# v of two batches loaded in four-token runs and unshuffled on TensorE, w_in in two halves, and a new order for slots 0 to 8

## The chip, the core and the metric

The kernel runs on one core of a Trainium2 chip. The engines of the core are TensorE (PE, with its weight loads shown as PEld), VectorE (DVE), ScalarE (ACT), GpSimd (POOL) and SyncE (SP), which here only issues transfers. Each engine has its own queue and works through it strictly in order; engines wait for one another and for transfers through semaphores. The metric is the device time in microseconds. Before the change it is 322.87 us, the median of three runs (322.14 to 323.13).

## The reference

Two layers run one after the other:

```
# q, k, v: (8 batches, 8 heads, 576 tokens, 64), fp32
scores = q @ k^T / 8 ; key j is seen by query i where 0 <= i - j < 128
scores += slope[h] * -(i - j)          # slope[h] = 2^-(h+1)
x = softmax(scores) @ v                # -> (4608 tokens, 512 = 8 heads * 64)
h = x @ w_in                           # w_in (512, 2048)
g = h * clip(h + 3, 0, 6) / 6
out = g @ w_out                        # w_out (2048, 512), out (4608, 512) fp32
```

## The kernel before

**Slots.** Attention is worked in 32 slots: slot g is batch g // 4 and head pair g % 4. Tokens lie in five blocks of 128 (the last has 64). For a slot, TensorE forms transposed scores for the diagonal blocks (`scd`) and for the blocks one off the diagonal (`sco`); ScalarE takes the exponential into `pd` and `po`; TensorE multiplies these by v, which has a column of ones beside each head (`vbuf`, 65 columns a head), so that one result holds both the weighted sum and its divisor; VectorE divides (`avs`); and five transposes with a copy put the slot into `xT`, the input of the second layer. In batch 0 the bias and the mask are added as table matmuls (`tables_diag`, `tables_off`) and `exp_full` takes 1024 columns at once; in later slots a bias column and a GpSimd select do this work, wholly or in part. From slot 8 on all scores of a slot go to one tile `sce` in 64x64 quarters (`scores`, L364 and L372).

**Second layer.** The tokens are cut in nine tiles nt of 512. For each nt there are 16 "up" units (four 512-column matmuls against `w_in`, L501, then ScalarE at L520 and VectorE at L521) and 16 "down" units (four 512-column matmuls against `w_out`, L551; four units make 128 rows of the output). `fill(n)` emits the next n units of a fixed list, if their tokens are in `xT`.

**PSUM.** There are eight banks: two tiles of two banks (`sc`), two tiles of one bank (`h`), one (`av`) and one (`o`). A tile can be written again only when its reader is done.

**Loading.** q and k of batch 0 come as nine-token runs (2304 bytes, `load_run`, L92), of batches 1 and 2 likewise (`load_double`, L98). v comes by tokens (`load_tokens`, L112): a descriptor for each token and head, 256 bytes. SyncE issues these in order, with eight completion lanes; a ninth transfer waits for the first. `w_in` comes through GpSimd's queue as four column quarters of 512 (`load_w_in`, L166), `w_out` as four row quarters (`load_w_out`, L171). Both are cast to bf16 on the way. Up unit ms needs w_in's columns 128 ms to 128 ms + 127.

**Order.** Everything is recorded by hand with `tc.manual_schedule`: `first_batch`, `second_batch`, then `segment(2 * NP, G)`, one slot an iteration. What stands in an engine's queue is the order of these calls. In `first_batch`, slots 0 to 3 go through transposes, scores and exponentials, then v is cast to bf16 (`cast_v`, L181), then `attend` (values of the slot in one `sc` tile) and `back` follow slot by slot; the first up units and the transposes of batch 1 (`wide_double`, L254) come after.

Of the kernel before, what the change touches and what calls it, by code (L numbers as in the profile page):

```python
# [18 lines left out]
def kernel(  # L19
# [29 lines left out]
    NB_FULL = 2  # L49
    RING = 4 * S  # L50
# [5 lines left out]
    ident = perm.tile([128, 128], BF16)  # L56
    bias3 = perm.tile([128, 1], FP32)
# [22 lines left out]
    p4buf = [held.tile([128, 2, 128], BF16, name=f"p4buf{i}") for i in range(2)]  # L80
# [94 lines left out]
    def second_w_in():  # L175
        nc.gpsimd.memset(w_out_sb[:, 4, 0:1], 0.0)
        load_w_in(1)

# [24 lines left out]

    def prepare(g, copies):
        for nm, copy in zip("qk", copies):
            pr = prs.tile([128, RT * D], BF16, tag=f"pr{nm}", name="pr",
                          padded_shape=[128, 2 * RT * D])
            copy(out=pr, in_=runs[nm][:, g % NP, :])
            st[g, nm] = pr

    def transposes(g, copies):
        b, hp = divmod(g, NP)
        for nm, dst, copy in (("q", qTb[b % 2], copies[0]), ("k", kTb[b % 2], copies[1])):
            src = st.pop((g, nm))
            tp = ps_h.tile([128, RT, RP], BF16, tag="h", name="tp", padded_shape=[128, 16, 64])
            for t in range(RT):
                for e in range(2):
                    r = slice(e * D, (e + 1) * D)
                    nc.tensor.transpose(tp[r, t, :], src[r, ts(t, D)], ident[r, r])
            copy(out=dst[:, hp, :, :].rearrange("p j c -> p (j c)")[:, 0:S].rearrange(  # L220
                "p (a t) -> p a t", t=RT), in_=tp.rearrange("p t a -> p a t"))
# [52 lines left out]
    def rooms(g):  # L274
        b, hp = divmod(g, NP)
        if full(g):
# [66 lines left out]
    def scores(g):  # L343
        if full(g):
            scores_diag(g)
            scores_off(g)
            return
# [4 lines left out]
        if g == 2 * NP:  # L352
# [31 lines left out]
    def exp_diag(g, e):  # L384
        h = 2 * (g % NP) + e
        pd = st[g, "pd"]
        if not full(g):
            nc.scalar.activation(out=pd[:, e, :, :], in_=st["sce"][e][:, :, 0, :],  # L388
                                 func=ACT.Exp, bias=bias_d[:, h:h + 1], scale=scale)
            mask_diag(g, e)  # L390
            return
        sc = st[g, "scd"]
        if diag_tabled(g):
            if e == 0:
                nc.scalar.activation(out=pd.rearrange("p e j c -> p e (j c)"), in_=sc,
                                     func=ACT.Exp, scale=scale)
            return
        nc.scalar.activation(out=pd[:, e, :, :].rearrange("p j c -> p (j c)"),
                             in_=sc[:, e, :], func=ACT.Exp,
                             bias=bias_d[:, h:h + 1], scale=scale)  # L400
        mask_diag(g, e)

    def mask_diag(g, e):
        pd = st[g, "pd"]
        nc.gpsimd.affine_select(out=pd[:, e, :, :], in_=pd[:, e, :, :],  # L405
                                pattern=[[0, 4], [1, 128]], channel_multiplier=-1, base=0,
                                compare_op=ALU.is_ge, fill=0.0)

    def exp_off(g, e):
        h = 2 * (g % NP) + e  # L410
        po, sc, p4 = st[g, "po"], st["sce"][e], p4buf[g % 2]
        nc.scalar.activation(out=po[:, e, :, :], in_=sc[:, :, 1, :], func=ACT.Exp,  # L412
                             bias=bias_o[:, h:h + 1], scale=scale)
        nc.gpsimd.affine_select(out=po[:, e, :, :], in_=po[:, e, :, :],  # L414
                                pattern=[[0, 4], [-1, 128]], channel_multiplier=1, base=-1,
                                compare_op=ALU.is_ge, fill=0.0)
        nc.scalar.activation(out=p4[:, e, 0:64], in_=sc[:, 3, 1, 64:128], func=ACT.Exp,  # L417
                             bias=bias_d[:, h:h + 1], scale=scale)
        if e == 1:
            nc.gpsimd.affine_select(out=p4[:, :, 0:64], in_=p4[:, :, 0:64],  # L420
                                    pattern=[[0, 2], [1, 64]], channel_multiplier=-1, base=0,
                                    compare_op=ALU.is_ge, fill=0.0)

    def av_matmuls(g, qts, where):
        b, hp = divmod(g, NP)
        vb = vbuf[b % 2]
        pd, po, p4 = st[g, "pd"], st[g, "po"], p4buf[g % 2]
        for qt in qts:
            for e in range(2):
                h = 2 * hp + e  # L430
                out_av = where(qt, e)
                if qt > 0:
                    nc.tensor.matmul(out_av, lhsT=po[:, e, qt % 4 if full(g) else qt - 1, :],  # L433
# [129 lines left out]
    ORDER = [("UUDUDUUDUD", "UUDUDUDUD", "UDUDUDD", "UUDDDD"),  # L563
# [3 lines left out]
    for nt in range(1, n_nt + 1):  # L567
        ups, downs = iter(range(16)), iter(range(16))
        for c in "".join(ORDER[0 if nt == 1 else 2 if nt == n_nt else 1]):
# [38 lines left out]
    def first_batch():  # L608
        prepare(0, (V, A))
        warm_up(20)  # L610
        tables_diag(0)
        tables_off(0)
        warm_up(10)
# [54 lines left out]
    def second_batch():  # L668
# [12 lines left out]
        for i in range(4):  # L681
            load_w_out(i)
# [130 lines left out]
```

## Time and profile before

| what | time |
|---|---|
| median of three runs | 322.87 us |
| the profiled execution | 323.39 us |
| its span in the profile | 321.4 us |
| TensorE busy | 309.9 us (96%) |
| ScalarE, VectorE, GpSimd busy | 195.8, 173.6, 140.2 us |
| transfers | 51.90 MB, of them 118976 packets under 512 bytes |

The profiled execution lies 0.52 us above the median, and 2.0 us of it lie outside the span. A matmul's busy time overlaps its neighbour's: a 512-column matmul is shown with a mean of 380 ns, and a row of 48 of them lasts 10.36 us. Busy shares therefore hide time in which TensorE does not stream at its full rate, and distances between starts are the better measure. A timeline row has start, duration, engine, line, operation, output and inputs, and in brackets the idle time before it with what ended it.

### The profile page before, as it was taken

To read this page: it belongs to the slowest core of one execution; us is meant where nothing else is said; L and a number is where in the kernel's file an instruction comes from. 1 tells how busy PE (TensorE), PEld (TensorE's weight loads), DVE (VectorE), ACT (ScalarE), POOL (GpSimd) and SP (SyncE) were. 2 spreads that over 40 slices of the span, in tenths; PEclk is the share of its full clock that TensorE was granted. 3 is DMA by queue.
4 is the path that set the end of the run, shared out by engine and by line. 5 is a ranking of instruction groups with operands and counts; after the bars stand their busy time and mean duration, and the time that the engine had idled before them with its cause. 6 is when DMAs were issued, how large, how long until landed. Compare 5 with 4: busy or idle time off the path is not lost.

```text
span 321.4 us, 7126 instructions
## 1 busy us (share of the span) xinstructions
PE 309.9 (96%) x2776; PEld 164.8 (51%) x2776; DVE 173.6 (54%) x338; ACT 195.8 (61%) x334; POOL 140.2 (44%) x249
## 2 busy tenths in 40 slices
PE   7879898999999999999999999999999999999996
PEld 6555455454554454444677654444444444444443
DVE  6757565664445555655565546554655455455510
ACT  4748876877777766766676667666764344244401
POOL 7455295586393866276645662763331000000000
PEclk9999999999999999999999999999999999999999
DMA  7999999999999999999999999942212200000112
GB/s 269 205 319 200 233 274 185 234 241 210 201 248 169 217 198 217 196 222 216 208 202 203 228 182 191 246 78 86 23 55 66 73 34 35 33 33 35 65 53 77
DMA packets 131425, 51.90 MB, mean 161 GB/s; under 512 B 118976, under 2 KB 123328, under 8 KB 131392
## 3 DMA queue, kind: packets, MB, share of 16 engines
q1 hardware_dynamic: 126160, 45.36, 66.4%
q0 software_dynamic: 4224, 4.19, 8.4%
q10 hardware_dynamic: 1008, 1.90, 1.6%
q8 instruction: 21, 0.34, 0.5%
q14 instruction: 12, 0.10, 0.1%
HBM read 36.70 MB, written 9.44 MB: 144 GB/s over the span
## 4 chain that ended last, share of the span: by engine, by line
PE 84%; DMA 7%; SPq 3%; POOL 2%; ACT 1%; issue 1%; DVE 1%; ACTq 0%; POOLq 0%
PE ops L551 38%; PE hps L501 36%; DMA ldbuf<-in_q_dram 3%; PE sce L364 3%; PE av L441 2%; DMA w_in_sb<-in_moe_w_in_dram 2%; SPq L112 2%; PE av L433 2%; DMA ldbuf<-in_k_dram 2%; SPq L98 1%; PE ops L532 1%; POOL w_out_sb L171 1%; PE tp L242 1%; POOL pr L227 1%; ACT r L520 0%
## 5 line engine op out<-in xcount | busy, mean ns | idle before, releaser
L521 DVE SCALAR_TENSOR_TENSOR gbuf<-r,hps 128x512 bf16<-128x512 f32 x144 | 98.8, 687 | 102.2 <-ACT r L520 100.9
L520 ACT ACTIVATE r<-hps,bias 128x512 f32<-128x512 f32 x144 | 98.9, 689 | 88.6 <-PE hps L501 88.3
L501 PE MATMUL hps<-xT,w_in_sb 128*128 128x512 bf16 (+1 forms) x640 | 144.9, 358 | 1.7 <-DMA w_in_sb<-in_moe_w_in_dram 1.5
L551 PE MATMUL ops<-w_out_sb,gbuf 128*128 128x512 bf16 x560 | 137.9, 380 | 0.0
L501 PEld LDWEIGHTS <-w_in_sb 128*128 128x128 bf16 x640 | 59.1, 98 | 56.7 <-DMA w_in_sb<-in_moe_w_in_dram 2.3
L551 PEld LDWEIGHTS <-gbuf 128*128 128x128 bf16 x560 | 51.8, 98 | 56.4
L414 POOL TENSOR_SCALAR_AFFINE_SELECT po<-po 128x512 bf16<-128x512 bf16 x48 | 30.2, 633 | 32.7 <-ACT po L412 32.5
L405 POOL TENSOR_SCALAR_AFFINE_SELECT pd<-pd 128x512 bf16<-128x512 bf16 x48 | 29.6, 631 | 31.6 <-ACT pd L388 31.6
L388 ACT ACTIVATE pd<-sce,bias_d 128x512 bf16<-128x512 f32 x48 | 31.6, 683 | 5.4 <-PE sce L372 5.4
L194 POOL CAST tbuf<-ldbuf 128x512 bf16<-128x512 f32 (+1 forms) x45 | 25.5, 611 | 18.6 <-DMA qTb<-tbuf 9.4
L560 DVE COPY osb<-ops 128x512 f32<-128x512 f32 x33 | 22.7, 688 | 20.0 <-PE ops L551 19.9
L412 ACT ACTIVATE po<-sce,bias_o 128x512 bf16<-128x512 f32 x48 | 32.9, 686 | 0.0
L452 DVE TENSOR_TENSOR avs<-av,rc 128x384 bf16<-128x384 f32 (+1 forms) x48 | 23.6, 491 | 1.6
L441 PEld LDWEIGHTS <-pd 128*128 128x128 bf16 x192 | 14.3, 97 | 8.3 <-POOL tbuf L194 0.5
L433 PE MATMUL av<-vbuf,po 128*128 128x65 bf16 x192 | 18.0, 193 | 0.0
L441 PE MATMUL av<-vbuf,pd 128*128 128x65 bf16 x192 | 17.3, 194 | 0.3 <-ACT kTb L244 0.3
L187 POOL CAST vbuf<-ldbuf 128x1024 bf16<-128x1024 f32 x14 | 14.2, 1041 | 5.4 <-DMA ldbuf<-in_v_dram 5.4
L433 PEld LDWEIGHTS <-po 128*128 128x128 bf16 x192 | 14.3, 98 | 2.9 <-DVE avs L452 0.5
L227 POOL CAST pr<-ldbuf 128x576 bf16<-128x576 f32 x20 | 12.8, 668 | 6.0 <-DMA ldbuf<-in_k_dram 3.8
L417 ACT ACTIVATE p4buf<-sce,bias_d 128x64 bf16<-128x64 f32 x48 | 15.4, 321 | 0.0
L364 PE MATMUL sce<-qTb,kTb 64*64 64x192 bf16 (+1 forms) x368 | 11.9, 246 | 0.0
L364 PEld LDWEIGHTS <-kTb 64*64 64x64 bf16 x368 | 7.1, 106 | 8.6 <-issue 8.5
(104 smaller groups left out, 207.8 us busy)
## 6 DMA issues: line engine op xcount, KB each, us to landing
out_dram<-osb SPq DMA_DIRECT2D x33, 256.0 KB, 2.4
ldbuf<-in_v_dram SPq DMA_DIRECT2D x32, 256.0 KB, 5.1
ldbuf<-in_q_dram SPq DMA_DIRECT2D x20, 256.0 KB, 4.8
ldbuf<-in_k_dram SPq DMA_DIRECT2D x16, 256.0 KB, 4.5
ldbuf<-in_q_dram SPq DMA_DIRECT2D x12, 288.0 KB, 7.5
ldbuf<-in_k_dram SPq DMA_DIRECT2D x12, 288.0 KB, 7.8
w_in_sb<-in_moe_w_in_dram POOLq DMA_DIRECT2D x4, 512.0 KB, 9.6
w_out_sb<-in_moe_w_out_dram POOLq DMA_DIRECT2D x4, 512.0 KB, 10.2
```

The source lines that it names most:

```text
L194: nc.gpsimd.tensor_copy(out=tbuf[:m, :, j, :], in_=s[:m, j, :, :].rearrange("p (i e) d -> p i (e d)", e=2))
L364: nc.tensor.matmul(sce[e][lo:lo + 64, j, :, :].rearrange("p s c -> p (s c)")[:, ds(lo, n)], lhsT=kT[r, j, lo:lo + 64], rhs=qT[r, ds(128 * ...
L388: nc.scalar.activation(out=pd[:, e, :, :], in_=st["sce"][e][:, :, 0, :], func=ACT.Exp, bias=bias_d[:, h:h + 1], scale=scale)
L405: nc.gpsimd.affine_select(out=pd[:, e, :, :], in_=pd[:, e, :, :], pattern=[[0, 4], [1, 128]], channel_multiplier=-1, base=0, compare_op=AL ...
L412: nc.scalar.activation(out=po[:, e, :, :], in_=sc[:, :, 1, :], func=ACT.Exp, bias=bias_o[:, h:h + 1], scale=scale)
L414: nc.gpsimd.affine_select(out=po[:, e, :, :], in_=po[:, e, :, :], pattern=[[0, 4], [-1, 128]], channel_multiplier=1, base=-1, compare_op=A ...
L433: nc.tensor.matmul(out_av, lhsT=po[:, e, qt % 4 if full(g) else qt - 1, :], rhs=vb[:, qt - 1, h, :], start=True, stop=False)
L441: nc.tensor.matmul(out_av, lhsT=d, rhs=vb[:, qt, h, :], start=(qt == 0), stop=True)
L501: nc.tensor.matmul(hps[:, lo:hi], lhsT=w_in_sb[:, ks, ts(ms, 128)], rhs=xT[:, ks, ds(src, hi - lo)], start=(ks == 0), stop=(ks == n_ks - 1))
L520: nc.scalar.activation(out=r6, in_=hps, func=ACT.Relu, bias=bias3[:, 0:1], scale=1.0 / 6.0)
L521: nc.vector.scalar_tensor_tensor(out=gts[nt][:, ms, :], in0=r6, scalar=1.0, in1=hps, op0=ALU.min, op1=ALU.mult)
L551: nc.tensor.matmul(ops[nt, sub], lhsT=gts[nt][:, ms, ts(sub, 128)], rhs=w_out_sb[:, ms, :], start=(ms == 0), stop=(ms == n_ms - 1))
```

## The change

The three functions that ordered slots 0 to 8 by loops are replaced by a written list of steps, `PLAN`, with one step a line, which `run_plan` emits in that order. It reaches to slot 19; the loop `segment` goes on from slot 20 as before. From slot 10 on the list has the order of work of the old loop. Up to slot 9 it is new:

* v of batches 0 and 1 is loaded in runs of four tokens (1024 bytes a descriptor; `s_ldv`), the last 64 tokens by tokens (`s_ldl`). Partition p then holds tokens 4p to 4p + 3 of the first 512. `s_cr` casts this to bf16 on GpSimd (`vruns`, in the room of `tbuf`), and `s_vp` puts the tokens in order: block j is the sum of four matmuls with 32 rows (partitions 32j to 32j + 31) and 512 columns against a selection matrix `sel`, into one bank; two blocks alternate in one step. `s_ve` copies a bank into `vbuf`.
* w_in comes as two column halves of 1024 (`s_wp`, one transfer each) where it was four quarters. The first half serves up units 0 to 7.
* Blocks 0 to 3 and block 4 of batch 0's values are kept apart, in `avs0`, in room of `gbuf`: a slot's first three blocks (`s_vf`), block 3 of three slots (`s_vr 0 3 3`), slot 3 whole (`s_vl`), block 4 of two slots (`s_vr 0 2 4`, `s_vr 2 2 4`). Four transposes a slot go back to `xT` (`s_bf`, `s_ef`), the four block-4 transposes together (`s_br`, `s_er`).
* Slots 8 and 9 form their scores like slots 4 to 7, without tables (`QF = 10`). `p4buf` has four buffers where it had two.
* Up and down units, loads and casts of batches 1 to 3 are placed one by one. Loads of q for batch 3 start before those of v for batch 2.

In the list the first word names the step: `c0` cast a run, `t0` transpose it, `e0` copy it out, `td` and `to` tables, `sd` and `so` scores, `xt`, `xo`, `xd`, `xf`, `x4` exponentials, `md`, `mf`, `m4` selects, `pd`, `dt`, `de` cast, transposes and copy for a double run, `nf`, `nr`, `nl`, `nv`, `na` division, `va` and `at` values, `bk` and `ek` back, `ub` and `u` the matmuls of an up unit, `ur` and `um` its ScalarE and VectorE parts, `d` a down unit, `dc` and `ds` copy and store of its rows, `ldd`, `ldt` loads by double run and by token block, `ct` the cast of a token block, `xb` and `bx` a transposing transfer, `mem` and `gl` small fills, `vt` the cast of v by tokens, `wu` warm-up matmuls. The last letter is the engine of a copy: V, P (GpSimd) or A.

```diff
-    def first_batch():  ...
-    def second_batch():  ...
+    SEL = sel[:, 0:4 * 129].rearrange("p (t c) -> p t c", t=4)
+    def s_ldv(b, h, n):
+        nc.sync.dma_start(out=vsource(b)[0][:, ds(h, n), :],
+                          in_=v[b, ds(h, n), 0:512, :].rearrange("h (p t) d -> p h (t d)", t=4))
+    def s_ldl(b):
+        nc.sync.dma_start(out=vsource(b)[1],
+                          in_=v[b, :, 512:S, :].rearrange("h p d -> p h d"))
+    def s_cr(b, h, n, eng):
+        C[eng](out=vruns[:, :, ds(h, n), :].rearrange("p t h d -> p h t d"),
+               in_=vsource(b)[0][:, ds(h, n), :].rearrange("p h (t d) -> p h t d", t=4))
+    def unshuffle(b, h, n, j0, banks):
+        for t in range(4):
+            for i, ps in enumerate(banks):
+                r = slice(32 * (j0 + i), 32 * (j0 + i) + 32)
+                nc.tensor.matmul(ps, lhsT=SEL[r, t, 0:128], rhs=vruns[r, t, ds(h, n), :],
+                                 start=(t == 0), stop=(t == 3))
+    def s_vp(b, j0, t1, t2):
+        banks = [psum(t, 512).rearrange("p (h d) -> p h d", h=H) for t in (t1, t2)]
+        ...
+        unshuffle(b, 0, H, j0, banks)
+    def s_wp(i, k0, n):
+        nc.gpsimd.dma_start(out=w_in_sb[:, ds(k0, n), ts(i, 1024)],
+                            in_=moe_w_in[ds(k0 * 128, n * 128), ts(i, 1024)].rearrange(
+                                "(k p) f -> p k f", p=128))
+    def s_br(tag):
+        tp = st["br"] = psum(tag, NP * 128, BF16).rearrange("p (g c) -> p g c", g=NP)
+        for g in range(NP):
+            nc.tensor.transpose(tp[:, g, :], avs0[:, g, 4, :, :].rearrange("p e d -> p (e d)"),
+                                ident)
+    def s_ub(nt, ms, n, tag):
+        hps = psum(tag, 512)
+        up_mms(nt, ms, 0, n, hps)
+        st["u", nt, ms] = hps, n
+    def run_plan(text):
+        for line in text.split("\n"):
+            if line.strip():
+                name, *args = line.split()
+                STEPS[name](*(int(a) if a.isdigit() else a for a in args))
+    PLAN = """
+ldv 0 4 4
+wu 20
+td 0
+c0 0 k P
+td 1
+wu 7
+ldv 0 0 4
+c0 0 q P
+c0 1 k A
+t0 0 q h
+e0 0 q V
+t0 0 k h
+t0 1 k o
+c0 1 q P
+mem 1
+e0 0 k A
+sel
+c0 2 q P
+e0 1 k A
+mem 0
+t0 1 q av
+e0 1 q V
+c0 2 k V
+ldl 0
+sd 0
+cr 0 0 4 P
+xt 0
+t0 2 q av
+c0 3 q V
+sd 1
+cr 0 4 4 P
+ldd 1 0 q 1
+t0 2 k h
+e0 2 k V
+ldd 1 0 k 0
+wp 0 0 4
+xt 1
+mem 2
+e0 2 q V
+to 0
+so 0
+xo 0
+t0 3 q o
+e0 3 q A
+td 2
+c0 3 k V
+sd 2
+xt 2
+td 3
+t0 3 k o
+to 1
+so 1
+e0 3 k V
+sd 3
+xo 1
+vp 0 0 av o
+xt 3
+vp 0 2 h h
+ve 0 0 8 2 1 A
+ldd 1 0 q 0
+mem 6
+to 2
+so 2
+to 3
+ve 0 0 8 1 1 A
+xo 2
+ve 0 0 8 0 1 V
+vf 1 av
+ve 0 0 8 3 1 V
+pd 1 0 q 0 V
+pd 1 0 q 1 P
+so 3
+xo 3
+nf 1
+pd 1 0 k 0 V
+dt 1 0 q 0 9 sc
+cl 0 P
+ldd 1 0 k 1
+pd 1 0 k 1 P
+vf 0 av
+nf 0
+ldd 1 1 q 1
+vr 0 3 3 o
+nr 0 3 3
+vf 2 h
+dt 1 0 k 0 9 sc
+de 1 0 q 0 9 A
+nf 2
+de 1 0 k 0 9 A
+bf 1 h
+bf 0 av
+ldd 2 0 k 1
+ef 1 0 512 V
+vl 3
+nl 3
+ldd 1 1 q 0
+sd 4
+bf 2 h
+ef 2 0 512 V
+ef 0 0 512 A
+to 4
+xd 4 0
+xd 4 1
+vr 0 2 4 av
+nr 0 2 4
+bf 3 h
+vr 2 2 4 h
+nr 2 2 4
+so 4
+md 4 1
+pd 1 1 q 0 P
+ldd 1 1 k 0
+ef 3 0 256 A
+md 4 0
+ef 3 256 256 A
+sd 5
+xo 4
+mem 7
+xd 5 0
+md 5 0
+br av
+u 0 7 o
+er V
+u 0 3 h
+ldv 1 0 4
+ur 0 7
+ur 0 3
+pd 1 1 k 0 V
+um 0 7
+xd 5 1
+u 0 4 av
+um 0 3
+ur 0 4
+um 0 4
+u 0 2 h
+pd 1 1 q 1 A
+ldd 1 1 k 1
+ur 0 2
+um 0 2
+u 0 1 h
+ur 0 1
+um 0 1
+ldd 2 0 k 0
+pd 1 1 k 1 P
+dt 1 1 k 0 9 sc
+wp 1 0 4
+md 5 1
+de 1 1 k 0 9 V
+cr 1 0 4 P
+u 0 5 av
+ur 0 5
+wout 2
+um 0 5
+dt 1 1 q 0 9 sc
+u 0 0 o
+ldv 1 4 4
+cr 1 4 4 P
+de 1 1 q 0 9 A
+ur 0 0
+um 0 0
+u 0 6 h
+to 6
+ur 0 6
+wout 0
+mem 3
+um 0 6
+mem 4
+sd 6
+xd 6 0
+so 6
+xo 6
+md 6 0
+vp 1 0 av h
+ve 1 0 8 1 1 V
+xd 6 1
+vp 1 2 h o
+pd 2 0 k 0 P
+ve 1 0 8 0 1 V
+to 7
+ve 1 0 8 3 1 A
+ldl 1
+cl 1 P
+wout 1
+ve 1 0 8 2 1 A
+sd 7
+so 7
+ldt 3 q 4
+u 0 15 h
...
+sd 8
+xd 8 1
+so 8
...
+u 1 2 h
+u 1 4 o
+xd 8 0
...
+mf 8 1
+xd 9 1
...
+d 0 0 0 h
+vt 2 2
+u 1 7 o
+ur 1 7
+mf 8 0
+va 8 0 3
+pd 2 1 q 0 P
+pd 2 1 q 1 P
+nv 8 0 3
+d 0 0 1 h
+d 0 0 2 h
+d 0 0 3 h
+um 1 7
+x4 9 1
+xd 9 0
+pd 2 1 k 1 A
+dc 0 0 V
+dt 2 1 k 0 5 o
+de 2 1 k 0 5 A
+dt 2 1 q 5 9 h
+dt 2 1 q 0 5 sc
+dt 2 1 k 5 9 av
+u 1 10 h
+ldt 2 v 4
+d 0 2 0 o
+ldd 3 0 k 1
+xf 9 0
+ldd 3 1 k 0
+md 9 1
+ct 3 q 0
+ct 3 q 1
+ct 3 q 2
+de 2 1 k 5 9 A
+ct 3 q 3
+ds 0 1
+ct 3 q 4
+xb 3 q
+pd 3 0 k 0 P
+de 2 1 q 0 5 V
+ds 0 0
+ldt 3 v 2
+vt 2 4
+m4 8
+de 2 1 q 5 9 V
+va 8 3 2
...
+"""
...
-        load_tokens(0, "v")
         constants()
         memsets()
-        memsets_later()
-        first_batch()
-        second_batch()
-        fill(2)
-        segment(2 * NP, G, lambda g: FILLS.get(g, (1, 1, 1, 2, 0, 1, 2)))
+        run_plan(PLAN)
+        done[0] = 20 - 1
+        segment(20, G, lambda g: FILLS.get(g, (1, 1, 1, 2, 0, 1, 2)))
```

More of the change, by code (lines that the diff above doesn't have):

```diff
@@ L202 @@
     st = {}
[L204 to L221, printed above, removed]
+    avs0 = gbuf[0].rearrange("p m c -> p (m c)")[:, ds(11 * NT, NP * NQ * 128)].rearrange(
+        "p (g j e d) -> p g j e d", g=NP, j=NQ, e=2)
     def prepare_double(b, dp, copies, nms="kq", early=None):
@@ L343, in scores @@
     def scores(g):
-        if full(g):
+        if g < QF:
             scores_diag(g)
@@ new lines @@
+xf 9 0
[17 more added lines that the diff above has]
+va 8 3 2
+sq 10
+ur 1 10
+pd 3 0 k 1 V
+um 1 10
+dt 3 0 k 0 5 h
+ldd 3 1 k 1
+nv 8 3 2
+de 3 0 k 0 5 A
+ldt 3 v 1
+bx 8
+u 1 12 h
+ur 1 12
+ldt 3 v 3
+ldt 3 v 4
+ldt 3 v 0
+um 1 12
+dt 3 0 k 5 9 h
+md 9 0
+mf 9 1
+de 3 0 k 5 9 A
+xd 10 0
+m4 9
+mf 9 0
+md 10 0
+d 0 2 1 o
+xd 10 1
+pd 3 1 k 0 A
+md 10 1
+va 9 0 3
```

1006 lines of the change are left out of this document (850 added, 156 removed).

## The prediction

> **What bounds the kernel now.** I read the page first, then busy time by stretches, then the timelines of TensorE, SyncE and GpSimd over the first 70 us.
>
> ```profile
> span 321.4 us, 7126 instructions
> PE 309.9 (96%) x2776; PEld 164.8 (51%) x2776; DVE 173.6 (54%) x338; ACT 195.8 (61%) x334; POOL 140.2 (44%) x249
> PE   7879898999999999999999999999999999999996
> DMA  7999999999999999999999999942212200000112
> ```
>
> TensorE is the bound, and the transfers are busy beside it for two thirds of the span. "96%" flatters TensorE, so I count what it streams. The rate comes from the end of the chain of waits, where nothing else runs:
>
> ```profile
> 304.46 10.36 PE ops L551 x48
> ```
>
> 48 matmuls of 512 columns in 10.36 us are 0.216 us each. From starts in the timeline a 128-column transpose takes 0.056, a 65-column value matmul 0.030, and two matmuls on different 64-row halves run side by side (eight of L296 take 0.22). Adding this up over all 2776 matmuls, 296.8 us are streamed and some 24 us of the span are lost: 3.2 in the first 8 us, 11.2 from 8 to 64, 2.6 from 64 to 96, 4.3 from 96 to 304 (0.2 in each 8 us), the rest at the end. Only the first 96 us hold much, and that is the part the change rewrites.
>
> ```profile
> 8.00:64.00 56.00, 50.35 (x637) 29.30 (x636) 34.98 (x56) 42.04 (x62) 30.38 (x49) 1.00 1.09 235
> 64.00:96.00 32.00, 31.42 (x309) 16.46 (x307) 15.77 (x32) 23.06 (x44) 21.98 (x39) 1.00 1.07 226
> 96.00:304.00 208.00, 208.00 (x1641) 106.91 (x1640) 114.96 (x216) 124.60 (x222) 81.60 (x144) 1.00 0.69 135
> ```
>
> The columns are span, then busy time of PE, PEld, DVE, ACT and POOL, granted clock, share of the transfers, GB/s. The clock is full; in the first two stretches the transfers are saturated (1.09, 1.07). What TensorE waits for there:
>
> ```profile
> 20.70 0.44 PE L482 MATMUL tb<-ident,avs 128*128 128x128 bf16 x5 [0.18 <-ACT xT L488]
> 21.34 0.90 PE L501 MATMUL hps<-xT,w_in_sb 128*128 128x512 bf16 x3 [0.20 <-DMA w_in_sb<-in_moe_w_in_dram]
> 22.07 0.44 PE L482 MATMUL tb<-ident,avs 128*128 128x128 bf16 x5
> 23.39 0.68 PE L254 MATMUL tp<-ident,pr 128*128 128x128 bf16 x9 [0.88 <-POOL pr L227]
> ```
>
> Each link of batch 0 waits for a copy, then the casts of batch 1 are late, then w_in's quarters (up units 4 and 8 start at 28.80 and 35.83 after waits on them). The loads are late because of this:
>
> ```profile
> 4.84 7.56 SPq L112 DMA_DIRECT2D ldbuf<-in_v_dram  x5
> 12.51 1.42 SPq L98 DMA_DIRECT2D ldbuf<-in_k_dram  x2
> 18.07 12.19 SPq L112 DMA_DIRECT2D ldbuf<-in_v_dram  x5
> ```
>
> The five v loads hold SyncE's queue for 7.56 and 12.19 us.
>
> **The change, part by part.** I take positions in the program from the written steps and durations from rows of the profiled execution (323.39 us, 0.52 above the median 322.87). Differences are worked out on its span and applied to the median.
>
> *Loads of v.* Packets of 256 bytes take 18 ns, of 2304 bytes 93 ns (228 and 396 GB/s over 16 engines). No row has 1024 bytes; bounds are 46 ns (on the line between the two) and 72 (four of 256). I take 46, since v's new packet is a plain longer one: 4096 x 18 / 16 = 4.6 us become 1024 x 46 / 16 = 2.9 a batch, 3.4 us of transfer time in two batches (none at the other end). It counts where a load is late. v of batch 0 lands near 11.7 us where the last cast waited to 15.9.
>
> *Unshuffling.* 16 matmuls of 512 columns a batch, 32 new in all: 6.9 us alone, 3.5 us if two neighbours on different 32-row strips pair like the 64-row halves of L296. That row is nearest in form, so 3.5. Eight bank copies at 0.64 us (four on ScalarE, four on VectorE) replace ten casts (five of 0.36 to 0.62 in batch 0; three of 1.04 and 0.61 on GpSimd in batch 1, which now does four `cr` of 1.04 and two `cl`).
>
> The Trainium skill (TensorEngine Tiling (Array Packing), Key Properties) says that changing the tiling mode drains TensorE. Here the start of L296 stands 0.1 us behind the transposes before it (26.35 + 9 x 0.056, then 26.95), so two entries and exits would cost 0.4 us; with 0.4 us each, as in PEld's 8.5 us over 21 waits at L364, it would be 1.6.
>
> *First up unit.* I followed the queues with those rows. GpSimd now casts both first runs, k then q (4.85 to 6.2), so the first scores come at about 8.2 us where they came at 6.88. Exponentials (1.02 each) and `e0` copies then alternate on ScalarE: the third `xt` ends at 13.3, `so 1` and `sd 3` at 14.3, where v's cast is also done (11.7 + 2 x 1.04). First `vp` 14.3 to 15.2. From there VectorE is the path: two `ve`, two `pd`, three `nf` (0.75), three `nr` (0.6 to 0.75), two `ef` (0.42), one `nl` (0.9): 8.9 us of work that starts at 15.2 and, with one gap for `vf 1`, ends at 24.9; `br` follows, and the first up unit starts at 25.3. Before, it started at 21.34, but by 25.3 the plan has done 2.2 us that stood later (slot 4, `sd 5`, two transposes of nine) and 1.7 of `vp`. So nothing is won up to here; some 0.1 to 0.5 is lost.
>
> The first half of w_in must be there by 25.3. It is issued at 13.8 (after v's casts). Quarters landed 7.3, 9.6 and 11.2 us after issue (least, median, most); the `w_out` quarters, nearly alone on the rings from 44 to 54 us, ran at 0.15 MB a us. Bounds: 1.05 MB / 0.15 + 2 us of start = 22.8, and two medians, 33. I take 24, as SyncE's queue stands still from about 11 to 17.8 (`ldd 2 0 k 1` waits for `pd 1 0 k 1`), so there is little to share with.
>
> *Up units 0 to 7* (to `u 0 15`): TensorE 8 x 0.864 + 1.0 transposes + 1.9 scores and tables + 1.7 `vp` = 11.6 us; ScalarE 11.8 by rows, 10.7 when back to back (two of L520 take 1.28). Equal, so TensorE sets it and 0.7 us of waits come on top: `u 0 15` at 37.5. The second half of w_in, issued near 28 behind `pd 1 1 k 1`, lands near 36. Before, the same work without `vp` was done at 36.8 (35.83 plus slot 7's 0.95).
>
> *Up units 8 to 15, first downs.* TensorE 25.0 us to `d 0 0 0`, ScalarE 24.3 (22 back to back). I find waits of 0.5 at `to 5` and of some 0.7 near `at 5` and `d 0 1 1`. Then `d 0 0 3` ends at about 68.3. Before, the same work (57.0 us streamed without `vp`, less 1.2 for warm-up matmuls at half rate) was done at 70.3. So 2.0 us are won there, by fewer waits.
>
> *Slots 8 and 9.* `xd 8 0` is placed late, and GpSimd then has 9.5 us in a row (`md`, two `mf`, two `vt`, three `pd`, five `ct`, `m4 8`) before `va 8 3 2`, 9.0 us later on TensorE: a wait of 0.8. It takes the place of waits from 70 to 96 us that amount to 1.9 above the usual 0.2 in 8. With 0.6 for late loads, 0.5 is won. The moved loads of q (batch 3, 256-byte packets) go ahead of v of batch 2; by 68 us 16.1 MB must have come, and 16.4 came before, so cover is thin.
>
> *Later.* Slots 10 to 19 keep their order; nothing there is priced but TensorE's own stream, which stays. The end is unchanged.
>
> Sum: -2.0 - 0.5 = -2.5. On the profiled execution 323.39 becomes 320.9, on the median 322.87 becomes 320.4.
>
> **The rivals.** (a) The first half of w_in is late, and the time ends on the other side. One transfer of twice the size that shares the rings takes two medians: it lands at 33, at worst, instead of 24. It decides from 25.3 + 2.5 = 27.8 on; at 31 it costs 5.7, 326. For it: quarters needed 7 to 11 us. Against: SyncE's pause.
> By a rule of the Trainium skill (DMA: Bandwidth & Descriptors, on arbitration) each engine goes round its queue rows packet by packet. Longer packets then take a larger share, which speaks for 24; no trace of before shows it at this size.
>
> (b) The strips do not pair, or each change of tiling costs. `vp` takes twice as long: 1.6 on the path before `to 2` and 1.7 before `u 0 15`, 323.7. For it: no row has 32 rows. Against: L296.
>
> (c) GpSimd or the loads hold slots 8 and 9 longer: a token block of 256 KB took 4.5 to 5.1 us to land, and `vt 2 4` stands behind such blocks. 2.5 more, 322.9: the change gives no gain.
>
> (d) The in-order chains overlap better than the rows say (two VectorE operations of 0.69 take 1.28) and waits up to `u 0 7` shrink by 3: 317.4.
>
> **How the numbers follow.** Forecast 0.50, (a) 0.12, (b) 0.10, (c) 0.13, (d) 0.15. Forecast and (d) are faster, and a third of (c); the measurement cannot tell less than 0.3% (1.0 us). Faster: 0.46 + 0.15 + 0.04 = 0.65; same: 0.03 of the forecast + 0.05 of (c) = 0.08; slower: 0.12 + 0.10 + 0.04 + 0.01 = 0.27. The likeliest case gives 320.4, with a range of its own of 318.5 to 321.9. The range reaches below to (d), 317.0, and above takes in (c), (b) and the milder half of (a), 325.0.
>
> **What would show it.** Right: first scores near 8.2, first up unit at 25 to 26 with no wait on w_in, up unit 15 at 37 to 38.5, the fourth part of `d 0 0` ending at 67 to 69.5, matmuls of an unshuffle starting in pairs (16 in about 1.75 us). Wrong: a wait of TensorE for w_in over 1 us, (a); starts 0.216 apart in the unshuffle, (b); TensorE waiting over 2 us for `vbuf` or selects of slots 8 and 9, (c); a first up unit before 23.5, (d). If the stretch from 96 to 304 loses more than 4.3 us, the forecast fails at a step that I priced at nothing.

## The result, and the profile after

The changed kernel takes 324.03 us, the median of 20 runs (323.01 to 324.55); the kernel before, run beside it, takes 322.66 (20 runs, 320.99 to 324.03). The ratio is 1.0051 with a 95% interval of 1.0037 to 1.0065. The change makes the kernel slower by 1.4 us, where 2.5 us of gain were forecast: the time lies in the range of the forecast, on the wrong side of the time before.

The page of the changed kernel, in the lines that were shown of before:

```profile
span 321.5 us, 7123 instructions
PE 306.9 (95%) x2763; PEld 166.7 (52%) x2801; DVE 177.3 (55%) x354; ACT 199.8 (62%) x343; POOL 133.9 (42%) x239
PE   7799899999989999999999999999999999999995
DMA  7999999979999979999999999942112200000111
```

and its three stretches (span, busy time of PE, PEld, DVE, ACT and POOL, granted clock, share of the transfers, GB/s):

```profile
8.00:64.00 56.00, 51.55 (x667) 31.03 (x670) 38.71 (x72) 45.46 (x70) 25.15 (x41) 1.00 1.06 246
64.00:96.00 32.00, 30.36 (x299) 17.07 (x303) 17.40 (x36) 24.12 (x45) 21.39 (x38) 1.00 1.04 216
96.00:304.00 208.00, 205.26 (x1614) 106.94 (x1639) 114.58 (x214) 124.48 (x222) 82.15 (x145) 1.00 0.66 133
```

The page hardly tells the kernels apart: the span is 321.5 us against 321.4. (Some records of matmuls are missing here, 2763 for 2801 weight loads, so less busy time in the last line is not more waiting; and a row of three matmuls behind "issue" is a unit of four whose first record is missing.) What tells them apart is TensorE's timeline, row by row (start, duration, line, operation, count, and in brackets the wait before it):

```profile
7.67 0.40 PE L279 MATMUL scd<-qTb,kTb 64*128 64x128 bf16 x8
...
15.52 1.07 PE L900 MATMUL bank<-tbuf,sel 32*128 32x512 bf16 x16 [0.45 <-POOL tbuf L893]
...
25.73 4.34 PE L459 MATMUL bank<-xT,w_in_sb 128*128 128x512 bf16 x19
...
34.84 1.61 PE L900 MATMUL bank<-tbuf,sel 32*128 32x512 bf16 x16
...
38.71 1.47 PE L459 MATMUL bank<-xT,w_in_sb 128*128 128x512 bf16 x5 [1.13 <-DMA w_in_sb<-in_moe_w_in_dram]
```

The first scores come at 7.67 us (forecast 8.2), the first unshuffle at 15.52 (14.3), the first up unit at 25.73 with no wait (25.3). The rows fit so far. Then `u 0 15` waits 1.13 us for the second half of w_in and starts at 38.71 (37.5). And here, in slots 11 to 13, is a stretch that the forecast had priced at nothing (the two L347 rows with 16 matmuls are the scores of slots 12 and 13):

```profile
85.75 1.89 PE L818 MATMUL bank<-w_out_sb,gbuf 128*128 128x512 bf16 x8
87.48 0.44 PE L765 MATMUL bank<-ident,avs 128*128 128x128 bf16 x5
87.85 0.52 PE L347 MATMUL sce<-qTb,kTb 64*64 64x192 bf16 x16
...
88.56 0.81 PE L818 MATMUL bank<-w_out_sb,gbuf 128*128 128x512 bf16 x3 [0.16 <-issue]
89.20 0.23 PE L399 MATMUL av<-vbuf,pd 128*128 128x65 bf16 x2
...
90.85 0.20 PE L391 MATMUL av<-vbuf,po 128*128 128x65 bf16 x1 [1.18 <-DVE avs L959]
...
91.20 0.69 PE L347 MATMUL sce<-qTb,kTb 64*64 64x192 bf16 x16
```

TensorE has nothing from 89.5 to 90.85: the second half of slot 11's values needs the bank that VectorE has yet to empty, and VectorE empties it late, because the copy of a down unit's rows stands ahead:

```profile
89.41 0.69 DVE L824 COPY osb<-bank 128x512 f32<-128x512 f32 x1 [2.81 <-PE bank L818]
90.01 0.18 DVE L958 RECIPROCAL rc<-av 128x6 f32<-128x6 f32 x1
90.23 0.56 DVE L959 TENSOR_TENSOR avs<-av,rc 128x384 bf16<-128x384 f32 x1
```

The scores of slot 13, which follow, find ScalarE at the last exponentials of slot 12 until 91.35; that adds some 0.2 us (the row of 91.20 lasts 0.69 us where 0.52 is usual). At the same point of the work, the kernel before has three down units where the changed one has one (a unit is four matmuls of L551), and its scores of slot 13 start at 91.47:

```profile
87.55 0.52 PE L364 MATMUL sce<-qTb,kTb 64*64 64x192 bf16 x16
87.88 0.21 PE L372 MATMUL sce<-qTb,kTb 64*64 64x64 bf16 x4
88.03 1.90 PE L551 MATMUL ops<-w_out_sb,gbuf 128*128 128x512 bf16 x8
89.77 0.23 PE L441 MATMUL av<-vbuf,pd 128*128 128x65 bf16 x2
...
90.07 1.03 PE L551 MATMUL ops<-w_out_sb,gbuf 128*128 128x512 bf16 x4
91.12 0.20 PE L433 MATMUL av<-vbuf,po 128*128 128x65 bf16 x1
...
91.47 0.52 PE L364 MATMUL sce<-qTb,kTb 64*64 64x192 bf16 x16
```

The unit between the two value steps covers VectorE's 1.2 us there. Counted from the values of slot 10 on, it is five units against three: the new list has used two more ahead of that point.

**A measure for all runs.** To place gains and losses I add up, from the end backwards, what TensorE still has to stream at each start (with the intervals from the prediction, warm-up and unshuffle left out), and ask at which time another kernel has the same remainder. Its *lead* is how much earlier that is than in the first profile of before, the one on which the forecast was summed. It is worked out from records of TensorE alone. Where the two kernels stand at different work, as they do around slots 11 to 13, the reading at one time depends on the intervals by some tenths. So in the columns of slots I compare at the same step: how much earlier its scores start, plus 0.864 us for each unit, and 0.056 for each transpose, that the kernel has done more by then. The rows above give the first profile: at the scores of slot 12 the changed kernel has done two units more, 87.55 - 87.85 + 2 x 0.864 = 1.43; at those of slot 13 both have done the same, 91.47 - 91.20 = 0.27.

| lead in us, at | 36 us | 64 us | scores of slot 12 | of slot 13 | of slot 14 | 312 us |
|---|---|---|---|---|---|---|
| forecast | | about 2.0 | | | 2.5 | 2.5 |
| changed, first profile | -0.60 | 0.82 | 1.43 | 0.27 | 0.41 | 0.16 |
| changed, second profile | -0.88 | 0.39 | 0.99 | -0.16 | -0.03 | -0.31 |
| before, second profile | 0.82 | 1.43 | 1.42 | 1.42 | 1.42 | 1.43 |
| before, third profile | 0.77 | 0.59 | 0.57 | 0.58 | 0.57 | 0.58 |
| before, fourth profile | 1.25 | 1.87 | 1.88 | 1.88 | 1.87 | 1.88 |

The measure agrees with the times: 323.39 less the lead at the end gives 321.96, 322.81 and 321.51 for the three later profiles of before, whose runs took 321.89, 322.55 and 321.24 us.

### The profile page after: what moved, and what is told of

The parts are those of the page before. It is cut to its first block, busy times and chain, and to the rows that moved or that the text cites. A ratio compares the mean times of both kernels' runs of the same rounds, so it can differ in the third digit from the quotient of the medians.

```text
span 321.5 us, 7123 instructions
## 1 busy us (share of the span) xinstructions
PE 306.9 (95%) x2763; PEld 166.7 (52%) x2801; DVE 177.3 (55%) x354; ACT 199.8 (62%) x343; POOL 133.9 (42%) x239
## 4 chain that ended last, share of the span: by engine, by line
PE 84%; DMA 10%; DVE 2%; issue 2%; POOL 1%; ACT 1%; SPq 0%; POOLq 0%
PE ops L509 24%; PE hps L459 22%; PE bank L459 14%; PE bank L818 12%; DMA ldbuf<-in_k_dram 4%; PE sce L347 3%; DMA w_in_sb<-in_moe_w_in_dram 3%; DMA ldbuf<-in_v_dram 3%; PE av L399 2%; PE av L391 2%; DMA xT<-avs 1%; PE ops L490 1%; PE bank L509 1%; PE bank L783 1%; POOL tbuf L893 1%
## 5 line engine op out<-in xcount | busy, mean ns | idle before, releaser
L478 ACT ACTIVATE r<-hps,bias 128x512 f32<-128x512 f32 x83 | 57.1, 688 | 64.8 <-PE hps L459 63.7
L479 DVE SCALAR_TENSOR_TENSOR gbuf<-r,hps 128x512 bf16<-128x512 f32 x83 | 57.1, 688 | 59.4 <-ACT r L478 58.5
L509 PE MATMUL ops<-w_out_sb,gbuf 128*128 128x512 bf16 x354 | 87.5, 379 | 1.5 <-issue 1.0
L459 PE MATMUL hps<-xT,w_in_sb 128*128 128x512 bf16 (+1 forms) x390 | 82.6, 344 | 0.3
L459 PE MATMUL bank<-xT,w_in_sb 128*128 128x512 bf16 x234 | 59.1, 379 | 1.8 <-DMA w_in_sb<-in_moe_w_in_dram 1.1
L811 DVE SCALAR_TENSOR_TENSOR gbuf<-r,bank 128x512 bf16<-128x512 f32 x61 | 41.3, 686 | 30.4 <-ACT r L806 30.0
L806 ACT ACTIVATE r<-bank,bias 128x512 f32<-128x512 f32 x61 | 41.7, 694 | 22.5 <-PE bank L459 22.2
L818 PE MATMUL bank<-w_out_sb,gbuf 128*128 128x512 bf16 x173 | 43.2, 379 | 1.0 <-issue 1.0
L658 ACT ACTIVATE pd<-sce,bias_d 128x512 bf16<-128x512 f32 x44 | 28.8, 683 | 5.4 <-PE sce L355 2.7
L518 DVE COPY osb<-ops 128x512 f32<-128x512 f32 x21 | 14.4, 688 | 17.3 <-PE ops L509 17.3
L399 PEld LDWEIGHTS <-pd 128*128 128x128 bf16 x192 | 14.3, 97 | 7.6
L391 PEld LDWEIGHTS <-po 128*128 128x128 bf16 x192 | 14.3, 98 | 3.7 <-DVE avs L959 1.3
```

Of the source, the lines that this page charges most:

```text
L391: nc.tensor.matmul(out_av, lhsT=po[:, e, qt % 4 if g < QF else qt - 1, :], rhs=vb[:, qt - 1, h, :], start=True, stop=False)
L399: nc.tensor.matmul(out_av, lhsT=d, rhs=vb[:, qt, h, :], start=(qt == 0), stop=True)
L459: nc.tensor.matmul(hps[:, lo:hi], lhsT=w_in_sb[:, ks, ts(ms, 128)], rhs=xT[:, ks, ds(src, hi - lo)], start=(ks == 0), stop=(ks == n_ks - 1))
L478: nc.scalar.activation(out=r6, in_=hps, func=ACT.Relu, bias=bias3[:, 0:1], scale=1.0 / 6.0)
L479: nc.vector.scalar_tensor_tensor(out=gts[nt][:, ms, :], in0=r6, scalar=1.0, in1=hps, op0=ALU.min, op1=ALU.mult)
L509: nc.tensor.matmul(ops[nt, sub], lhsT=gts[nt][:, ms, ts(sub, 128)], rhs=w_out_sb[:, ms, :], start=(ms == 0), stop=(ms == n_ms - 1))
```

## The experiments

**Both kernels once more.** The same two kernels, with no edit.

> The kernel before, unchanged, for a second profile. Theory A (the two kernels really differ by 1.4 us in the typical execution, and the first profile of the kernel before was a slow one): a span of 319.5 to 320.8, with less lost in the first 64 us than the 14.4 of the first profile. Rival B (the profiles are typical, the medians of other executions differ for reasons outside the trace): a span of 321.2 to 321.6 with the same losses at the same places.

> The changed kernel, unchanged, for a second profile and more times. Theory A (its typical execution loses more than the first profile shows, at waits for transfers): a span of 322.2 to 322.8, with the wait for the second half of w_in at 1.5 us or more, and the same gap of 1.8 us at slots 12 and 13. Rival B: a span near 321.5 with the wait at 1.1 again.

The kernel before took 321.89 us in the profiled run (span 320.0), the changed one 323.64 in 12 runs, ratio 1.0041 (1.0014 to 1.0068). The loss at slots 11 to 13 is there again, 1.15 us from the scores of slot 12 to those of slot 13 in both profiles, of which 0.14 come back by slot 14, and so is the wait for w_in (1.3 us). (The expectations below speak of 1.75 us at 88 to 92; that is the lead read at fixed times.) The kernel before is another matter: it stands 1.4 us ahead of its own first profile from 52 us on. Two further profiles, taken last, tell which is usual:

> The kernel before, a third profile. Theory A (the first profile, on which the sum was made, was a slow course of the first 64 us): it stands near the second, 1.0 to 1.5 us ahead of the first at the same remaining work from 52 us on, span 320.0 to 320.5. Rival (the second was a lucky one): within 0.5 us of the first, span 321 to 321.5.

> The kernel before, a fourth profile, as the third: near the second (theory A, span 320.0 to 320.5) or near the first (rival, 321 to 321.5).

They took 322.55 and 321.24 us, spans 320.9 and 319.5. Neither expectation holds: the third lies between the first and the second, the fourth ahead of all, and the four profiles of before lead by 0, 1.43, 0.58 and 1.88 us, all of it won before 64 us, and then keep their distance to 0.02 us. What differs is seen in the lists of what TensorE waits for (total, times, longest). The first profile:

```profile
PE hps L501 <- DMA w_in_sb<-in_moe_w_in_dram: 1.5, 3, 0.8
PE w L153 <- POOL ident masks.py:199: 1.4, 1, 1.4
PE tp L242 <- POOL pr L227: 1.0, 1, 1.0
PE tp L254 <- POOL pr L227: 0.9, 1, 0.9
```

and the fourth:

```profile
PE w L153 <- POOL ident masks.py:199: 1.4, 1, 1.4
PE scd L296 <- DVE kTb L220: 0.9, 3, 0.4
PE scd L296 <- ACT kTb L220: 0.7, 1, 0.7
PE tb L482 <- ACT xT L488: 0.6, 3, 0.2
```

The 1.5 us for w_in and the 1.9 for GpSimd's casts (`pr`), waits that end in transfers, are not in the fourth list at all. The casts in turn wait for loads (1.77 us for a load of k ahead of the cast at 20.98 in the first profile, 0.38 ahead of the same cast at 20.13 in the fourth). So these waits come and go from run to run with the landing of transfers.

**The unshuffle.** First, the order in which the strips follow one another: all four matmuls of one block, then those of the next, where the change alternates two blocks.

```diff
-        for t in range(4):
-            for i, ps in enumerate(banks):
+        for i, ps in enumerate(banks):
+            for t in range(4):
```

> The four matmuls of a block follow each other on the same 32 rows, so that no two neighbours lie on different rows. Theory A (the strips run side by side, and that is why 16 matmuls took 1.0 and 1.5 us): the 16 take about 3.5 us in each batch, starts 0.216 apart, and the time is 2 to 4 us longer, 326 to 328. Rival B (32 rows are streamed faster whatever the order): the 16 still take 1.0 to 1.7 us and the time stays within 0.5 us of the changed kernel.

323.35 us (10 runs), ratio to before 1.003 (1.0006 to 1.0054); not to be told from the changed kernel's 1.0041. The first unshuffle of this run:

```profile
15.53 1.08 PE L900 MATMUL bank<-tbuf,sel 32*128 32x512 bf16 x16 [0.62 <-POOL tbuf L893]
```

The next row starts at 16.54, so 16 matmuls of 512 columns take 1.01 us in this order as in the other (15.52 to 16.52). Starts come four to each 0.216 us: four strips run side by side whichever order they are issued in. It is not that 32 rows stream faster by themselves: in batch 1 of the changed kernel, as long as only the two strips of the first step are at work, starts come in pairs 0.216 to 0.226 us apart (34.84, 35.06, 35.28). And the strips do not wait for one another in the queue: the ninth of these 16 matmuls, the first of the second step (known by the wait that it carries), starts at 35.41, ahead of the last two of the first step (35.50).

Second, v by tokens again, in the new order (no run casts, no selection, no bank copies; the casts by tokens at the places of `cr` and `cl`):

```diff
-ldv 0 4 4
+ldt 0 v 0
+ldt 0 v 1
+ldt 0 v 2
 ...
-cr 0 0 4 P
+vt 0 0
 ...
-vp 0 0 av o
-vp 0 2 h h
-ve 0 0 8 2 1 A
 ...
```

> The new order with v of batches 0 and 1 loaded by tokens and cast on GpSimd as before; no unshuffling, no selection matrix. Theory A (the unshuffling pays for itself: its matmuls cost TensorE 2.5 us but v is there 3 to 4 us earlier, and the order was made for it): slower than the changed kernel by 1 to 4 us, 325 to 328, with TensorE waiting for vbuf before the values of slots 0 and 4. Rival B (the order carries what is won, and the unshuffling is a cost of 2.5 us of TensorE): faster by 1 to 2.5 us, 321.5 to 323.

328.43 us (4 runs), ratio 1.0181 (1.0142 to 1.0221): by the ratios 4.2 to 4.5 us above the changed kernel. TensorE's waits in this run begin so:

```profile
PE bank L459 <- DMA w_in_sb<-in_moe_w_in_dram: 4.0, 1, 4.0
PE wide L783 <- DVE rcn L698: 2.5, 1, 2.5
PE sco L290 <- ACT gbuf L359: 1.5, 1, 1.5
```

The size is about what theory A had, but not its wait: none of the listed waits is for vbuf. The longest is for the second half of w_in. In this order, with the casts at these places, the four-token runs are worth more than 4 us. That tells nothing of what they would be worth in the old order, which was not tried.

**The wait for w_in.** The second half issued some steps earlier, ahead of the exponentials of slot 5:

```diff
 mem 7
+wp 1 0 4
 xd 5 0
 ...
 dt 1 1 k 0 9 sc
-wp 1 0 4
 md 5 1
```

> The second half of w_in is issued before md 5 0 and pd 1 1 k 1 on GpSimd instead of after them, some 1 to 2 us earlier. Theory A (TensorE waits at up unit 15 because of the issue): the wait of 1.1 us is gone, 0.8 to 1.3 us faster than the changed kernel, 322.7 to 323.2. Rival B (the transfers are saturated: what w_in gains is lost by v and q behind it): within 0.4 us of the changed kernel, with a new wait of TensorE before 48 us or at slot 8.

322.73 us (12 runs), ratio 1.0001 (0.9981 to 1.0021). The wait for w_in is gone, and the lead at 64 us is 1.24. Then w_in in quarters again, at the places of the halves:

```diff
-wp 0 0 4
+win 1
+win 0
 ...
-wp 1 0 4
+win 3
+win 2
```

> The changed kernel with w_in in four quarters again, two issued where the first half was (the second quarter, which unit 7 reads, and then the first) and two where the second half was (the fourth, which unit 15 reads, and then the third). Theory A (the quarters of one queue land one after the other): the fourth quarter lands about half a transfer, 4 us, before the half did at 38.7, the wait of 1.1 us at unit 15 is gone, and the time falls by 0.4 as with the earlier half: 322.8. Rival (the two transfers share the 16 engines and land together, and GpSimd pays for two more issues): the wait stays and the time with it, 323.6 or some tenths above.

322.43 us (12 runs), ratio 1.0008 (0.9997 to 1.002). Unit 15 does not wait:

```profile
37.84 1.90 PE L459 MATMUL bank<-xT,w_in_sb 128*128 128x512 bf16 x7
```

The fourth quarter was issued at 30.36 us, later than the half of the changed kernel (30.03), and landed at 35.71, in time for unit 15; the third, issued at 31.12, landed at 39.13, where the half had landed at 38.66. So cutting the transfer in two does not bring all of it any sooner. What unit 15 gains is that it waits for one quarter, and for the one that goes first. The lead at 64 us becomes 1.69. Both ways bring the kernel back to the time before, and no further.

**The hole at 88 to 92 us.** Two down units of later slots drawn into it:

```diff
 m4 12
+d 1 1 0 o
 va 11 3 2
 nv 11 3 2
+d 1 1 1 o
 ...
-bk 11 o
+bk 11 h
 ...
 md 13 0
-d 1 1 0 o
 ...
 x4 13 0
-d 1 1 1 o
```

> Two down units (d 1 1 0 and d 1 1 1) moved from slot 13 up to the values of slot 11, and bk 11 put in an h bank. Theory A (the gain up to 88 us is given back at 88 to 92, where TensorE has no unit between the values of slot 11 and the scores of slot 13): 1.2 to 1.7 us faster than the changed kernel, 322.4 to 322.9, no gap there. Rival B (the gap is ScalarE's: the exponentials of slot 12 are the path, and the units only move the gap to slot 13): less than 0.4 us, 323.6 to 324.4, with a gap of over 1 us between 92 and 96.

323.96 us (12 runs), ratio 1.0037 (1.0017 to 1.0056): no gain. The hole closes in part: from the scores of slot 12 to those of slot 13 the lead falls by 0.44 us (0.94 to 0.50) instead of 1.15. But it goes on falling, and at the scores of slot 15 it is 0.11, as if almost nothing had been done. TensorE's timeline there:

```profile
90.64 1.02 PE L818 MATMUL bank<-w_out_sb,gbuf 128*128 128x512 bf16 x4 [0.47 <-DVE osb L824]
...
94.36 1.24 PE L459 MATMUL bank<-xT,w_in_sb 128*128 128x512 bf16 x5 [0.29 <-ACT xT L769]
96.23 1.89 PE L459 MATMUL bank<-xT,w_in_sb 128*128 128x512 bf16 x8 [0.33 <-DVE gbuf L811]
```

There is no gap of over 1 us between 92 and 96, as rival B had it. The units are missing one slot on, where up units now follow each other and wait, for `xT` and for a bank. Next, all later units of two token tiles shifted, so that no single slot would be short:

```diff
-"DDDDUUDUDUDUDUUDUDUDUDUUDUDUDDUU"   # order of units, token tile 2
+"DDDDDDUUUUDUDUUDUDUDUDUUDUDUDDUU"   # tiles 2 and 3
```

The units in the list follow this order; around the hole, unit 1 0 3 lies between the two halves of slot 11's values and two more down units behind them.

> d 1 0 3 behind va 11 0 3, two more down units (d 1 1 0, d 1 1 1) before the scores of slot 13, and every later slot gets as many units as it had, each two further on in the list. Theory A (what is lost at 88 to 92 us is a lack of units there, and in the earlier trial the hole only moved on, as the next slots had fewer): 0.8 to 1.5 us faster than the changed kernel, 322.4 to 323.2, and the lead at 104 us as large as at 88. Rival B (the slots' own chain of exponentials and selects sets the pace from slot 11 to 13): within 0.4 us of the changed kernel.

> e7_flow and the earlier issue of w_in's second half together. Theory A (the two losses are separate): the gains add, 1.8 to 2.6 us faster than the changed kernel, 321.2 to 322.0, a little faster than the kernel before. Rival B (they are one chain): no better than the better of the two, about 322.7.

(`e7_flow` is the shift of the units.) 326.6 us (1.0131, 1.0092 to 1.0169) and, with the second half of w_in early, 325.08 (1.0086, 1.0055 to 1.0116): worse by 3 and 1.4 us than the changed kernel. The edit was bad: it leaves four up units in a row in each tile, and TensorE waits for their banks and for `xT`:

```profile
PE bank L459 <- DVE gbuf L811: 1.3, 2, 0.6
...
PE hps L459 <- DMA xT<-avs: 1.1, 3, 0.4
```

The lead falls from 0 at the scores of slots 14 to 17 to -1.4 at those of slot 18, and to -2.6 at those of slot 30. The pair says that later units can't be had for nothing; it says nothing on the hole itself. So the units were left in their slots, and only the order around the hole was changed. First the scores of slot 12 alone, 2 us earlier:

```diff
 va 10 3 2
 nv 10 3 2
+sq 12
 d 1 0 1 o
 d 1 0 2 o
+xd 12 0
+md 12 0
 bk 10 h
 ek 10 A
-sq 12
 d 1 0 3 o
 dc 1 0 V
 ds 1 0
-xd 12 0
-md 12 0
```

(`xd 12 0` thus stands ahead of `ek 10` on ScalarE; the other exponentials of slot 12 follow as before.)

> The changed kernel with the scores of slot 12 moved ahead of two down units (1 0 1 and 1 0 2) and of the transposes of slot 10, and nothing else. In the profile of the changed kernel TensorE stands still from 89.5 to 91.2 us, and two things end there within 0.4 us of each other: the values of slot 11 (rows 3 and 4) wait for the VectorE row that empties their bank (90.8, behind the copy of down unit 1 0, 89.4 to 90.1), and the scores of slot 13 wait for ScalarE's exponentials of slot 12 (to 91.35). Theory A (both waits are to be moved, the hole comes of two down units that are missing there): the exponentials end 2 us earlier, the wait for VectorE stays 1.2 us, the gain is 0.2 to 0.4 us, 323.3. Theory B (the late scores alone make the hole, VectorE's row is late only because everything is): 1.5 us gained, 322.1, the time of before.

324.07 us (7 runs), ratio 1.0057 (1.0036 to 1.0077). Nothing is gained: the wait for VectorE is still 1.2 us, and from the scores of slot 12 to those of slot 13 the lead falls by 1.16 us, as in the changed kernel. The late scores were not the hole. Then the three down units laid singly:

```diff
 nv 10 3 2
+sq 12
 d 1 0 1 o
+...            # exponentials of slot 12 begin
-d 1 0 2 o
 bk 10 h
 ek 10 A
-sq 12
-d 1 0 3 o
-dc 1 0 V
 ...
 va 11 0 3
 nv 11 0 3
+d 1 0 2 o
 ...
 va 11 3 2
 nv 11 3 2
+d 1 0 3 o
+dc 1 0 V
```

> The changed kernel with the scores of slot 12 ahead of the down units 1 0 1, 1 0 2 and 1 0 3, and these three laid singly between the scores of slot 12, the values of slot 11 and the scores of slot 13, where they stand two ahead and one behind; same work, no other slot touched. Theory A (the loss at 88 to 92 us is a matter of the order there, and what is won stays won): both waits are covered by a down unit of 0.86 us each, some 1.5 us of the 1.75 are won, and nothing is given back later: 322.1 us, ratio to before near 1.000, the lead at 104 us some 1.9 instead of 0.4. Rival (the units are short, so that the hole moves on to slots 13 to 15, as it did where two later units were drawn into it): the lead at 92 is 1.8 and at 104 again 0.4; 323.5, ratio 1.004.

322.92 us (12 runs), ratio 1.0023 (1.0004 to 1.0042). TensorE's timeline around the hole:

```profile
86.40 0.52 PE L347 MATMUL sce<-qTb,kTb 64*64 64x192 bf16 x16
...
87.11 0.81 PE L818 MATMUL bank<-w_out_sb,gbuf 128*128 128x512 bf16 x3 [0.16 <-issue]
...
88.34 1.02 PE L818 MATMUL bank<-w_out_sb,gbuf 128*128 128x512 bf16 x4
...
89.64 1.03 PE L818 MATMUL bank<-w_out_sb,gbuf 128*128 128x512 bf16 x4
90.60 0.52 PE L347 MATMUL sce<-qTb,kTb 64*64 64x192 bf16 x16
```

Between the scores of slot 12 and those of slot 13 there is no wait on VectorE or ScalarE left. The lead is 0.87 at the scores of slots 12 and 13 and 0.83 at those of slot 14: 0.04 us lost where 1.0 were, and nothing is given back up to slot 21. In this profile the start had been slow (a wait of 1.5 us for w_in, lead 0.26 at 64), which is why the lead at 104 did not reach the 1.9 expected.

**Both mended.** The spread units with w_in's second half early, and with w_in in quarters:

> The same with the second half of w_in issued some steps earlier, ahead of the exponentials of slot 5, which took its wait of 1.1 us away. Theory A: both gains add up, 1.5 and 0.4 to 0.9: 321.2 to 321.7 us, ratio to before 0.997 to 0.9985. Rival (slots 13 to 15 take back what is won): 322.7, as the earlier half alone.

> The changed kernel with w_in in quarters at the places of the halves and with the scores of slot 12 ahead and its three down units laid singly. Theory A (these two losses are independent and nothing is given back): the gain of the quarters (1.2 us between medians of one job) and that of the spreading (1.1) add up, 321.1 us, ratio to before 0.9965. Rival (what stands ahead is caught up by a later wait): 322 us or more.

321.11 us (12 runs), ratio 0.9966 (0.9952 to 0.998), and 321.49 us (12 runs), ratio 0.9974 (0.9953 to 0.9995). (The 1.2 us of the second expectation lies between medians of two sets of runs, not of one.) Both beat the kernel before and the changed one. Within their intervals the gains add up. Against the kernel before in the same set of runs, the changed kernel takes 1.0041 to 1.0051, the earlier half alone 1.0001, the spreading alone 1.0023, and both 0.9966: gains of 0.40 to 0.50%, 0.18 to 0.28%, and 0.75 to 0.85% together. The profiles' spans are 319.8 us in both, with leads at 64 us, the scores of slots 12 and 14, and 312 us of 1.81, 2.42, 2.38, 1.89 and 1.45, 2.06, 2.03, 1.89.

## Why the prediction was wrong, by its own steps

*Loads of v; unshuffling: the packet was right, the landing late, the matmuls cheaper.* v's new packets of 1024 bytes took a median of 47 ns on SyncE's queue, for the 46 that I took (over 2048 packets in the trace of the changed kernel). (I wrote that no row of before has this size; its trace has 4096 such packets, at 96 ns, but they are those of w_in and w_out, which cast on the way.) Still, the half of v that is cast first landed at 13.39 us, where I had 11.7, and the first unshuffle came 1.2 us later than forecast. Against this, 16 matmuls took 1.0 us in batch 0 and 1.5 in batch 1 (34.84 to 36.38), 2.5 in all for the 3.5 that I took from the 64-row halves. The Trainium skill (TensorEngine Tiling (Array Packing), Theoretical Speedup) gives up to four times for 32 rows; the trace agrees, with four starts in each 0.216 us, or 0.054 us a matmul. Of its drain at a change of mode (Key Properties) there is at most 0.14 us here: 1.00 us less 16 x 0.054. Rival (b) is out.

*First up unit: right.* 25.73 us, no wait for the first half of w_in, no gain up to here: the lead at 24 us is about -0.7, the unshuffling not counted. The first half of w_in was issued at 15.41, 1.6 us later than forecast, and landed at 23.86, as I had it (24), because it took 8.45 us and not 10.2. Rival (a) did not come for the first half, nor did (d).

*Up units 0 to 7: failed, by the landing of w_in's second half.* I had it issued near 28 us, landed near 36, and needed at 37.5. The chain of waits shows what came (start, duration, what):

```profile
21.24 8.03 DMA ldbuf<-in_k_dram
...
29.43 0.52 POOL pr L774
...
30.03 8.63 DMA w_in_sb<-in_moe_w_in_dram
38.66 0.05 issue
```

A load of k that took 8.03 us held the cast ahead of it in GpSimd's queue; the half was issued at 30.03, 2.0 us later than forecast, and took 8.63 us, where I had 8. That is a wait of 0.9 to 1.5 us in every profile of this order. It is not rival (a)'s mechanism, a transfer of twice the size that takes two medians (19 us): the half took less than the 9.6 of one quarter of before. What failed is the time of issue, behind a load that came late. With the half issued earlier the ratio to before goes back to 1.0001, with the needed quarter first to 1.0008, so this term is shown.

*Up units 8 to 15: the 2.0 us were not all there.* The last part of `d 0 0` ended at 68.85 us against 68.3 forecast, but the lead was 0.82 and 0.39 in the two profiles, not 2.0. Over six profiles with the changed kernel's order up to 64 us and w_in's wait (two of itself, and the runs with the filled hole, the strips in a row, the scores up and the spread units) it is 0.82, 0.39, 0.34, 1.24, 0.10 and 0.26, a mean of 0.5 (the shift of the units, with some 0.4, leaves it so); over the five with w_in mended 1.24, 1.80, 1.69, 1.81 and 1.45, a mean of 1.6. The forecast of 2.0 for this order, against the profile of before that I summed on, is thus right within 0.4, once the wait for w_in is out.

*The base of the sum: failed.* "Differences are worked out on its span and applied to the median." The profile of before that I summed on was the slowest of four; their mean lead is 1.0. The waits of transfers and casts that the change was to remove are the very ones that vary, so its excess over the median lay in the terms that I counted as won. I kept them whole and moved the 0.5 us over as if they had nothing to do with them. Against the median of 322.66, the first profile of 323.39 makes 0.7 us of gain that was not to be had.

*Slots 8 and 9: right.* Between 64 us and the scores of slot 12 the changed kernel gains 0.6 us in both profiles, for the forecast 0.5. The parts were not all there: no wait for `va 8 3 2` is in the trace, where I had 0.8. Rival (c) is out.

*"Later": failed, by the largest of the terms, 1.3 us in two parts.* "Slots 10 to 19 keep their order; nothing there is priced." The order of attention is kept there, but not the units that lie in it: the list has used two more ahead of them, and between the scores of slot 12 and of slot 13 one is left where three had been. The waits that these had covered, VectorE's 1.2 us and some 0.2 for ScalarE's exponentials, come out, and 1.0 us is lost from the scores of slot 12 to those of slot 14, in both profiles of the changed kernel, and again in those with the strips in a row, with w_in early and with w_in in quarters. The spread units win all but 0.04 us of it back and keep it.

A further 0.25 and 0.29 us go at one place after the scores of slot 21. The chain of waits shows it in the first profile:

```profile
153.71 4.24 DMA xT<-avs
...
157.99 1.14 PE hps L459 x9
```

An up unit waits there in the middle of a row for a transfer that brings values into `xT`. In the four profiles of before this transfer took 2.37 or 2.38 us, in those of the changed kernel 4.24 and 4.27, and from 4.09 to 4.61 in the eight runs that keep the units of the later slots. Why it takes longer is not known.

The account: 2.5 forecast; less 1.1 for w_in and 0.4 for the rest up to 64 us; plus 0.1 in slots 8 and 9; less 1.0 at slots 11 to 13 and 0.3 later: -0.2 us on the first profile of before, whose excess of 0.7 over the median turns this into 0.9 us slower, of 1.4 measured. The remaining 0.5 us is not placed: the median of 324.03 lies above both profiles of the changed kernel (323.25 and 323.71), and no trace of a slower run was kept. That the time lies inside the stated range at all is luck: the upper end was set for rivals (a), (b) and (c), and none of them came.

## What to carry to other kernels

Where a list is rewritten up to some slot, look at the first slots behind it too: what they hold beside their own chain may have been used up ahead, and a wait that was covered there comes back at nearly its full price (1.15 of 1.2 us here). If a stage is said to keep its order, compare it instruction by instruction on the bounding engine, fillers too. And before waits on transfers are counted as a gain, take a second profile: here four profiles of one kernel differ by 1.9 us in just these waits, more than the 1.4 us of the change.

## What was not expected of the hardware

Four 32-row strips run fully side by side with 128 columns each, 16 matmuls of 512 columns in 1.0 us, and it does not matter whether neighbours in the queue lie on different strips (1.01 us with the same strip four times in a row). So inside TensorE a matmul does not wait for one ahead of it in the queue that lies on another strip: in batch 1 the ninth started before the seventh and the eighth.

Two transfers of half the size were no faster together than one (the second landed at 39.13 us, the single one at 38.66), but the first of them landed after 5.35 us where the single one took 8.63. That counts for a reader that needs only one part.
